# Score matmuls of two units issued together from unit 8 on, under a new written order

## The chip, the cores and the metric

The kernel runs on one core of a Trainium2 chip. The metric is the device time of one execution in microseconds, the median of several runs; a profile of one execution with its trace goes with it.

## The reference

The program computes a linear-attention recurrence and feeds its result to a two-layer perceptron. Inputs are r, k and v of shape (4 batches, 8 heads, 768 steps, 48), a decay w and a bonus u of shape (8, 48), and weights of 384 x 2048 and 2048 x 384.

```python
for t in range(S):
    cur = einsum('bhd,bhe->bhde', u * k_t, v_t)
    y_t = einsum('bhd,bhde->bhe', r_t, state + cur)
    state = w * state + einsum('bhd,bhe->bhde', k_t, v_t)
x = y as (4*768, 8*48)
h = x @ w_in
g = where(h >= 1, h, where(h <= -1, 0, (h + 1)**2 / 4))
out = g @ w_out
```

## The kernel before

**Tiling.** The 768 steps are cut into six chunks of 128. A unit is one chunk of one batch, all eight heads, so there are 24 units; unit i is chunk i // 4 of batch i % 4. Two units make a block (12 blocks), and a block's 256 rows go through the perceptron together: layer 1 in eight groups (`L1:m:n`, each two feature tiles of 128, so six matmuls of 256 columns), the activation `sm:m:n` on ScalarE (ACT), and layer 2 in eight steps for each of the two units (`L2:m:u:n`, two matmuls of 384 columns each), then the copy `oc:m:u` out of PSUM and the store `so:m:u`. The first two blocks run layer 1 by single units (`L1:m:n:u`, twelve matmuls of 128 columns).

**A unit's own work.** Loads `ld:K`, `ld:R`, `ld:V` (line 278) on the queue of SyncE (SP). K and R are weighed with powers of the decay (`Kw`, `Rw`, line 282) into one of five buffers. Both are transposed: by TensorE (PE) and a copy for units below 8 (`trp`, `trc`), by a DMA on SP's queue from unit 8 on (`tr`, line 315). `at:i` (function `scores`, line 317) makes the 128 x 128 scores of the eight heads: eight matmuls, alternating between partitions 0 to 47 and 64 to 111, of 48 rows each, into two PSUM tiles A0 and A1. `mk:i:0` and `mk:i:1` (line 326, VectorE, DVE) mask them into bf16. `y:i` multiplies the masked scores with V and, from the second chunk on, adds K/R's product with the carried state. The diagonal term of u is a product of K, u and R (`KU1`, `KU2`), a reduction to one number per head (`dg:i`, line 297) and eight multiply-adds in `x:i` (line 354, DVE; below unit 6 it is `VD` and one more matmul). `xp`, `xT` turn x for layer 1 (from unit 14 on by DMA). `st`, `Ta`, `Td`, `Tb` update the state for the unit four later. `xs` and `nsq`, `ns`, `nm`, `nx`, `flag` bound the range of h; if the bound fails, a slower exact path runs behind.

**PSUM.** There are eight banks: two for layer 1 (`ps_h`), two for layer 2 (`ps_o`), and four (`ps_a`) taken in turn by everything else: `trp`, `at` (two of them), `y`, `xp`, `st`. A tile takes the bank of the one allocated four before it, and its first matmul waits until that one has been read.

**What sets the order.** Each engine executes its instructions in the order in which they are written, and that order is a string, `ORDER`: its tokens are taken one after the other (line 638), each emits its operation on its engine, and `@DVE`, `@ACT`, `@POOL` behind a token moves it to another engine than its usual one (POOL is GpSimd). `warm*n` emits n idle matmuls that keep PE busy while it has nothing else to do. The table of `op(...)` calls carries estimated costs, needs and due times for a planner that wrote the string; when the kernel is built only the engine and the function of each are used. The weights come in quarters on POOL's queue (`gi`, `go`, lines 465 and 470), each held back by a small copy until a named load has landed; `li` and `lo` emit nothing.

In the order before, each unit's `at` stands alone, with one exception: `at:21 at:22` follow each other but for operations of other engines between them.

Of the kernel before, what the change touches and what calls it, by code (L numbers as in the profile page):

```python
# [16 lines left out]
w u ld:K:0 ld:K:1 ln warm*12 ub tab:K ld:R:0 Kw:0 wt uc ld:V:1 tab:R KU1:0 dec ld:R:1 gi:0 ld:V:0 Rw:0 KU2:0  # L17
warm*41 trp:0 ld:R:2 trc:0@DVE gi:1 li:0 dg:0 warm*11 at:0 Vb:0 mk:0:1 VD:0@POOL st:0 mk:0:0 gi:2 ld:K:2
Ta:0:1 warm*12 y:0 Ta:0:0 Tb:0:1 Rw:1 Tb:0:0 ld:V:2 Kw:1 x:0@DVE warm*17 xp:0 xs:0 li:2 gi:3 trp:1 xT:0
trc:1 Kw:2@DVE warm*2 L1:0:0:0 Rw:2 KU1:1@DVE sm:0:0:0 li:1 warm*7 at:1 KU2:1 mk:1:0 KU1:2 warm*7 L1:0:2:0  # L20
dg:1 mk:1:1 li:3 Vb:1 sm:0:2:0 trp:2 KU2:2@DVE trc:2 VD:1 st:1 dg:2 Vb:2 L1:0:1:0 Ta:1:0 ld:K:3 y:1 VD:2
sm:0:1:0 at:2 Ta:1:1 x:1 ld:K:4 mk:2:1 st:2 Tb:1:0 xs:1 L1:0:3:0 mk:2:0 ld:R:3 go:0 Tb:1:1 xp:1 Ta:2:0
sm:0:3:0 Ta:2:1 ld:V:3 warm*2 y:2 xT:1 Kw:4 x:2@DVE Tb:2:0 ld:R:4 Tb:2:1 go:1 warm*9 L1:0:1:1 xs:2 xp:2 lo:0
sm:0:1:1 L1:0:0:1 go:2 L1:0:2:1 sm:0:0:1 Rw:4 xT:2 L1:0:3:1 Kw:3 sm:0:2:1 lo:1 trp:4 sm:0:3:1 Rw:3@POOL
L1:1:0:0 trc:4@DVE L1:1:1:0 KU1:3 sm:1:0:0 L2:0:1:0 sm:1:1:0 L2:0:0:0 lo:2 go:3 at:4 L2:0:1:1 mk:4:1 KU1:4
L1:1:2:0 mk:4:0 trp:3 sm:1:2:0 KU2:4 L2:0:1:2 lo:3 L2:0:1:3 trc:3 L1:1:3:0 KU2:3 dg:4 sm:1:3:0 Vb:3 dg:3
warm*6 L2:0:1:4 L2:0:1:5 ld:K:5 L2:0:0:1 VD:3@POOL L2:0:0:2 at:3 ld:V:4 L2:0:0:3 mk:3:0 L2:0:0:4 st:3
L2:0:1:6 mk:3:1 ld:K:6 L2:0:1:7 KU1:5 L2:0:0:5 Ta:3:0 L2:0:0:6 Ta:3:1 ld:R:5 Tb:3:0 L2:0:0:7 Vb:4 oc:0:1 y:3
Tb:3:1 VD:4 L2:1:0:0 ld:V:5 x:3 L2:1:0:1 oc:0:0 xs:3 L2:1:0:2 Kw:5@DVE st:4 ld:R:6 y:4 Rw:5 xp:3 x:4
L2:1:0:3 KU2:5 Ta:4:1 ld:V:7 L2:1:0:4 xT:3@DVE xs:4 L2:1:0:5 Ta:4:0 trp:5 Vb:5 dg:5 ld:R:7 L1:1:2:1 Td:4  # L30
trc:5 VD:5 xp:4 ld:V:6 st:5 L1:1:0:1 Kw:6 xT:4@DVE sm:1:2:1 Ta:5:0 L2:1:0:6 Ta:5:1 ld:K:7 sm:1:0:1 at:5
Rw:6@DVE L1:1:3:1 Tb:4:0 KU1:6 mk:5:1 Tb:4:1 ld:R:8 L1:1:1:1 sm:1:3:1 mk:5:0 Td:5 trp:6 ld:K:8 sm:1:1:1
KU2:6@DVE L2:1:1:0 L2:1:0:7 Vb:6@ACT Vb:7 y:5 ld:K:10 trc:6 oc:1:0 Rw:7 L2:1:1:1 x:5@DVE L2:1:1:2 so:0:1
Tb:5:0 Kw:7 L2:1:1:3 dg:6 st:6 Tb:5:1 ld:K:9 L2:1:1:4 xs:5 Ta:6:1 xp:5 KU1:7 at:6 Ta:6:0 xT:5 so:0:0
L2:1:1:5 mk:6:1 L2:1:1:6 ld:V:8 Kw:8 L2:1:1:7 mk:6:0 st:7 L1:2:0 so:1:0 KU2:7 oc:1:1 L1:2:4 ld:R:9 sm:2:0
Ta:7:1 y:6 Td:6 Ta:7:0 sm:2:4 dg:7 L1:2:1 Rw:8 ld:V:9 Tb:6:1 L1:2:3 sm:2:1 KU1:8 x:6 so:1:1 L2:2:1:0 sm:2:3
trp:7 ld:R:10 L1:2:2 Tb:6:0 KU2:8 trc:7 L1:2:5 tr:8 Vb:8 dg:8 xp:6 sm:2:2 Td:7 L2:2:0:0 xT:6@DVE L2:2:0:1
sm:2:5 Rw:9@DVE at:7 ld:K:11 xs:6 st:8 Kw:9 L2:2:1:1 mk:7:1 L1:2:6 ld:R:11 mk:7:0 Kw:10 L1:2:7 sm:2:6 Ta:8:0
ld:V:10 L2:2:0:2 sm:2:7 KU1:9@DVE L2:2:0:3 y:7 Vb:9 Ta:8:1 tr:9 L2:2:1:2 KU2:9 Tb:7:1 x:7 L2:2:1:3 Tb:7:0
L2:2:0:4 L2:2:1:4 Td:8 L2:2:0:5 ld:R:13 L2:2:0:6 Rw:10 dg:9 xs:7 at:8 xp:7 ld:K:12 mk:8:1 L2:2:0:7 Vb:10  # L40
xT:7 L2:2:1:5 Kw:11 mk:8:0 st:9 L2:2:1:6 ld:V:11 L2:2:1:7 Ta:9:0 L1:3:1 Rw:11 Ta:9:1 ld:K:13 oc:2:1 y:8
sm:3:1 L1:3:0 KU1:10 oc:2:0 Tb:8:0 tr:10 x:8 L1:3:2 sm:3:0 KU2:10 at:9 Tb:8:1 L1:3:3 sm:3:2 Td:9 ld:R:12
dg:10 xs:8 L2:3:0:0 KU1:11 L1:3:4 mk:9:1 sm:3:3 ld:V:12 st:10 mk:9:0 Vb:11 xp:8 sm:3:4 L2:3:1:0 L1:3:5
KU2:11@DVE so:2:1 xT:8 Kw:12 Ta:10:0 ld:K:14 L2:3:0:1 sm:3:5 Ta:10:1 y:9 dg:11 L1:3:6 Td:10 Tb:9:0 tr:11 x:9
Tb:9:1 L1:3:7 Rw:12 sm:3:6 L2:3:1:1 sm:3:7 at:10 KU1:13 ld:V:13 L2:3:1:2 xs:9 mk:10:1 L2:3:0:2 Kw:13 xp:9
so:2:0 st:11 mk:10:0 L2:3:1:3 L2:3:1:4 ld:V:14 xT:9@DVE Vb:12 L2:3:0:3 Ta:11:1 L2:3:0:4 Rw:13 Ta:11:0 y:10
ld:R:14 L1:4:0 Tb:10:1 x:10 Td:11 Tb:10:0 L1:4:1 Vb:13 sm:4:0 tr:12 at:11 Kw:14 sm:4:1 L1:4:2 mk:11:1 xs:10
KU1:12 L2:3:0:5 ld:K:15 mk:11:0 L1:4:3 sm:4:2 KU2:12 st:12 xp:10 ld:R:15 sm:4:3 Ta:12:0 L1:4:5 Ta:12:1 xT:10
Rw:14 y:11 dg:12 ld:V:15 sm:4:5 L1:4:4 x:11 Tb:11:1 Td:12 L2:3:1:5 tr:13 sm:4:4 L1:4:6 Vb:14 Tb:11:0 KU2:13
L2:3:0:6 sm:4:6 at:12 L2:3:1:6 xs:11 tr:14 KU1:14 xp:11 dg:13 L1:4:7 xT:11 mk:12:1 KU1:15 L2:3:1:7 sm:4:7  # L50
L2:3:0:7 mk:12:0 ld:K:16 st:13 L1:5:0 Rw:15@DVE ld:R:16 L1:5:2 KU2:14 oc:3:1 sm:5:0 y:12 oc:3:0 sm:5:2
ld:V:16 L1:5:3 Kw:15 Ta:13:1 Tb:12:1 Ta:13:0 L2:4:0:0 sm:5:3 x:12 L2:4:0:1 so:3:1 Td:13 L2:4:0:2 so:3:0
Vb:15 at:13 Tb:12:0 ld:K:17 Kw:16 L1:5:1 mk:13:0 xs:12 L2:4:1:0 L2:4:1:1 Rw:16 dg:14 ld:V:17 sm:5:1 L2:4:1:2
mk:13:1 L2:4:1:3 L2:4:0:3 KU1:16 ld:R:17 L2:4:1:4 st:14 L1:5:4 Ta:14:1 KU2:15 ld:K:18 Ta:14:0 y:13 sm:5:4
at:14 Vb:16 x:13 tr:15 Tb:13:0 L2:4:1:5 Kw:17 Tb:13:1 L2:4:0:4 L1:5:5 mk:14:0 L2:4:0:5 Vb:17 xs:13 ld:R:18
L1:5:6 KU2:16 mk:14:1 sm:5:5 xp:13 L2:4:0:6 ld:V:18 dg:15 xT:13 xp:12 Td:14 L2:4:1:6 dg:16 sm:5:6 y:14 Rw:17
tr:16 L1:5:7 xT:12 x:14 Tb:14:1 KU1:17 L2:4:1:7 sm:5:7 st:15 st:16 L2:4:0:7 ld:K:19 Tb:14:0 KU2:17 L1:6:0
Ta:15:0 xs:14 oc:4:0 at:15 ld:R:19 KU1:18 oc:4:1 sm:6:0 L2:5:0:0 L1:6:1 Ta:15:1 xp:14 mk:15:0 L2:5:1:0 Td:15
sm:6:1 L1:6:2 mk:15:1 Kw:18 so:4:1 L2:5:1:1 sm:6:2 dg:17 L2:5:1:2 so:4:0 Vb:18 L2:5:1:3 Ta:16:1 ld:V:19 y:15
KU1:19 Ta:16:0 L2:5:0:1 Tb:15:1 x:15 at:16 Tb:15:0 ld:K:20 Rw:18 L1:6:3 L2:5:0:2 tr:17 sm:6:3 KU2:18@DVE  # L60
L2:5:0:3 L1:6:4 xs:15 Kw:19 mk:16:1 L2:5:0:4 nsq:0 dg:18 L2:5:1:4 xp:15 Td:16 L2:5:0:5 mk:16:0 st:17 KU2:19
sm:6:4 L1:6:5 Ta:17:0 tr:18 Ta:17:1 L2:5:1:5 sm:6:5 Vb:19 L2:5:0:6 ns:0 L1:6:6 Rw:19 ld:V:20 dg:19 y:16
sm:6:6 L2:5:1:6 Kw:20 x:16 L1:6:7 Tb:16:0 ld:R:20 Tb:16:1 L2:5:0:7 Td:17 sm:6:7 L2:5:1:7 KU1:20 at:17
ld:K:21 nsq:1 oc:5:1 st:18 L1:7:0 mk:17:0 oc:5:0@ACT ld:R:21 L1:7:1 mk:17:1 xs:16 Vb:20 st:19 L2:6:1:0 xp:16
# [36 lines left out]
def kernel(  # L101
# [126 lines left out]
    t = {}  # L228
# [461 lines left out]
```

## Time and profile before

| | |
|---|---|
| median of 5 runs | 182.57 us (182.2 to 183.2) |
| the profiled execution's own time | 183.74 us |
| its span | 181.8 us |
| PE busy | 168.9 us, 93% |
| DVE busy | 121.5 us, 67% |
| POOL busy | 108.4 us, 60% |
| ACT busy | 105.7 us, 58% |
| masks, A to AT (line 326) | 48 of 683 ns |
| x's multiply-adds (line 354) | 144 of 257 ns |
| score weight loads (line 322) | 192, PE idle 4.9 us in 17 places before them, released by nothing seen ("issue") |

The page divides the span into 40 slices and shows the busy share of each in tenths. Its chain of work follows the execution back from its last instruction to what released each step. The timeline lists neighbouring instructions of one kind as one row: start, length to the last one's end, and how often. Matmuls overlap, so the distance between two starts says more about what one costs than its own length. A wait's releaser is inferred; "issue" means that no other engine was seen to release it.

### The profile page before, as it was taken

The page shows a single profiled execution, that of the slowest core. Times are in us where ns is not written, and L with a number is a line of the kernel's source. Part 1 is how long each engine was busy: PE and PEld are TensorE (multiplying, and loading weights), DVE is VectorE, ACT ScalarE, POOL GpSimd, SP SyncE. Part 2 cuts the span into 40 slices and gives each one's busy share as a digit, 9 for nine tenths or more (in the row PEclk, how much of TensorE's full clock was granted, in tenths as well). Part 3 has the DMA queues.
Part 4 walks back from the last instruction along what each step waited for, and adds up shares of the span by engine and source line. Part 5 has one row for each costly group of instructions (what it writes and reads, how often), then busy time and mean ns, then how long its engine had stood idle before and what let it go on. Part 6 is the DMA issues. An engine that isn't in the chain of part 4 may idle for free.

```text
span 181.8 us, 4899 instructions
## 1 busy us (share of the span) xinstructions
PE 168.9 (93%) x1891; PEld 130.2 (72%) x1891; DVE 121.5 (67%) x330; ACT 105.7 (58%) x225; POOL 108.4 (60%) x151
## 2 busy tenths in 40 slices
PE   5987686999999999999999999999999999999970
PEld 3976576767878777787778777777777776877750
DVE  2257773559996999979868899889879674100220
ACT  3406296526869548588738568777947451764200
POOL 7787489663999697999988997932940000000000
PEclk9999999999999999999999999999999999999999
DMA  4999979999989799699999888979972032110221
GB/s 99 218 190 205 190 125 198 188 198 194 227 197 195 161 219 192 140 207 140 246 208 172 199 163 167 232 154 170 238 162 79 4 86 66 40 50 0 73 86 36
DMA packets 103424, 27.79 MB, mean 153 GB/s; under 512 B 96481, under 2 KB 103394, under 8 KB 103394
## 3 DMA queue, kind: packets, MB, share of 16 engines
q1 hardware_dynamic: 99538, 24.16, 65.6%
q0 software_dynamic: 3712, 3.15, 10.8%
q8 instruction: 17, 0.28, 0.7%
q14 instruction: 13, 0.11, 0.2%
q10 hardware_dynamic: 144, 0.10, 0.2%
HBM read 20.65 MB, written 4.72 MB: 139 GB/s over the span
## 4 chain that ended last, share of the span: by engine, by line
PE 80%; SPq 12%; DMA 4%; DVE 1%; issue 0%; ACT 0%
PE o_p L432 35%; PE h_p L401 32%; SPq L278 12%; PE A L322 4%; DMA R<-in_r_dram 4%; PE y L337 2%; PE y L334 2%; PE st L378 2%; PE tr L306 1%; PE xp L362 1%; DVE RKW L282 1%; PE y L343 0%; SPq L243 0%; PE n_p L488 0%; PE o_p L240 0%
## 5 line engine op out<-in xcount | busy, mean ns | idle before, releaser
L412 ACT ACTIVATE gT<-h_p 128x512 bf16<-128x512 f32 x96 | 56.8, 596 | 39.3 <-PE h_p L401 37.5
L401 PE MATMUL h_p<-xT,w_in_sb 128*128 128x256 bf16 (+1 forms) x672 | 75.1, 257 | 2.2 <-DMA w_in_sb<-in_moe_w_in_dram 1.8
L432 PE MATMUL o_p<-w_out_sb,gT 128*128 128x384 bf16 (+1 forms) x400 | 75.9, 320 | 0.0
L401 PEld LDWEIGHTS <-w_in_sb 128*128 128x128 bf16 x672 | 56.8, 98 | 12.6 <-DMA w_in_sb<-in_moe_w_in_dram 1.9
L432 PEld LDWEIGHTS <-gT 128*128 128x128 bf16 x400 | 36.4, 98 | 15.5
L326 DVE TENSOR_TENSOR AT<-A,umask 128x512 bf16<-128x512 f32 x48 | 31.3, 683 | 8.4 <-PE A L322 8.3
L354 DVE SCALAR_TENSOR_TENSOR x<-Vb,dg,y 128x48 bf16<-128x48 bf16 x144 | 26.7, 257 | 3.8 <-PE y L337 3.6
L182 DVE COPY o_sb<-o_p 128x384 f32<-128x384 f32 (+1 forms) x20 | 10.6, 541 | 19.9 <-PE o_p L432 19.7
L282 POOL TENSOR_TENSOR RKW<-K,Winv 128x384 bf16<-128x384 f32 x21 | 21.6, 1033 | 3.6 <-DMA K<-in_k_dram 1.9
L293 POOL TENSOR_TENSOR KU<-KU,R 128x384 f32<-128x384 f32 x20 | 20.2, 1014 | 4.3 <-DVE KU L290 2.8
L182 ACT CAST Tbd<-T 48x192 bf16<-48x192 f32 x40 | 13.9, 348 | 15.2 <-DVE T L386 10.2
L290 POOL TENSOR_TENSOR KU<-K,u_bc 128x384 f32<-128x384 f32 x22 | 21.9, 1000 | 0.0
L372 ACT ACTIVATE x<-x 128x384 bf16<-128x384 bf16 x24 | 12.5, 521 | 5.1 <-DVE x L354 3.7
L282 POOL TENSOR_TENSOR RKW<-R,Wpow 128x384 bf16<-128x384 f32 x14 | 14.0, 999 | 0.8 <-DMA R<-in_r_dram 0.8
L182 POOL CAST Vb<-V 128x384 bf16<-128x384 f32 x22 | 11.3, 517 | 5.2 <-DVE x L354 2.5
L282 DVE TENSOR_TENSOR RKW<-R,Wpow 128x384 bf16<-128x384 f32 x10 | 9.0, 897 | 7.4 <-DMA R<-in_r_dram 7.3
L297 DVE TENSOR_REDUCE dg<-KU 128x8 f32<-128x384 f32 x24 | 13.0, 545 | 1.4 <-POOL KU L293 1.3
L389 POOL TENSOR_TENSOR T<-T,wc 128x192 f32<-128x192 f32 x16 | 9.4, 590 | 6.1 <-DVE T L384 6.1
L384 DVE TENSOR_TENSOR T<-T,st 48x192 f32<-48x192 f32 x32 | 11.2, 350 | 2.6 <-PE st L378 2.1
L240 PE MATMUL w_p<-ident 128*128 128x128 bf16 x120 | 11.1, 261 | 0.0
L240 PEld LDWEIGHTS <-ident 128*128 128x128 bf16 x126 | 10.1, 119 | 0.3
L322 PEld LDWEIGHTS <-RK 48*128 48x128 bf16 x192 | 5.4, 94 | 6.0 <-issue 4.9
(74 smaller groups left out, 146.2 us busy)
## 6 DMA issues: line engine op xcount, KB each, us to landing
K<-in_k_dram SPq DMA_DIRECT2D x24, 192.0 KB, 3.7
R<-in_r_dram SPq DMA_DIRECT2D x24, 192.0 KB, 3.7
V<-in_v_dram SPq DMA_DIRECT2D x24, 192.0 KB, 4.0
out_dram<-o_sb SPq DMA_DIRECT2D x23, 192.0 KB, 2.2
w_in_sb<-in_moe_w_in_dram POOLq DMA_DIRECT2D x4, 384.0 KB, 7.8
w_out_sb<-in_moe_w_out_dram POOLq DMA_DIRECT2D x4, 384.0 KB, 8.1
RK<-RKW SPq DMA_TRANSPOSE x16, 3.9
w_bc<-in_w_dram SPq DMA_DIRECT2D x1, 192.0 KB, 3.6
```

What stands on the lines that cost most here:

```text
L182: (eng.copy if eng is nc.scalar else eng.tensor_copy)(to, src)
L240: mm(spare[0][:, d_out:], ident, ident, start=False, stop=False, skip_group_check=True)
L278: nc.sync.dma_start(out=t[name, i], in_=src[b, :, c * C : (c + 1) * C, :].rearrange("h s d -> s h d"))
L282: at_engine((name + "w", i)).tensor_mul(RKW[i % RING["W"]][:, off : off + H, 0:D], t[name, i], tab)
L290: at_engine(("KU1", i)).tensor_mul(t["KU", i], t["K", i], u3)
L293: at_engine(("KU2", i)).tensor_mul(t["KU", i], t["KU", i], t["R", i])
L297: nc.vector.reduce_sum(t["dg", i], t["KU", i], axis=AX)
L326: nc.vector.tensor_mul(t["AT", i, s], t["A", i][s], umask4)
L354: nc.vector.scalar_tensor_tensor(x[:, h * D : (h + 1) * D], t["Vb", i][:, h, :], t["dg", i][:, h : h + 1], t["y", i][:, h, :], op0=ALU.mul ...
L401: mm(h_p[:, f, :], w_in_sb[:, kk, (nf * n + f) * 128 : (nf * n + f + 1) * 128], xT[m][:, :, kk, :] if u_ is None else xT[m][:, u_, kk, :], ...
L412: nc.scalar.activation(g, h_p, AF.Square, bias=0.5, scale=0.5)
L432: mm(t["o", m, u, part_], t["g", m][:, f, u * C : (u + 1) * C], w_out_sb[:, f, e], start=(f == 0), stop=(f == nN - 1),)
```

## The change

Three edits outside the order, and a new order. `PAIR = 8` is added. From unit 8 on there is no `at` of a single unit: `at:8`, `at:10` and so on emit `scores` of a unit and of the next one (the two units of a block), sixteen matmuls into four PSUM tiles, so that they take the whole `ps_a` pool. `dg` gets 12 buffers instead of 4. The order is another string throughout.

```diff
-    PE_T, PE_X, PE_D, ONE = 8, 14, 6, 2
+    PE_T, PE_X, PE_D, ONE, PAIR = 8, 14, 6, 2, 8
...
-        t["dg", i] = work.tile([128, H], F32, name="dg", tag="dg", bufs=4)
+        t["dg", i] = work.tile([128, H], F32, name="dg", tag="dg", bufs=12)
...
+    RTs = {}
+    def at_key(i):
+        return ("at", i if i < PAIR else i - i % 2)
+
+    def scores_of_two(i):
+        scores(i)
+        scores(i + 1)
...
-        op(("at", i), "PE", 0.45, (scores, i), [RT], d + 3, [("a", [("mk", i, s)]) for s in range(2)])
+        RTs[i] = RT
+        if i < PAIR:
+            op(("at", i), "PE", 0.45, (scores, i), [RT], d + 3, [("a", [("mk", i, s)]) for s in range(2)])
+        elif i % 2:
+            op(at_key(i), "PE", 0.66, (scores_of_two, i - 1), [RTs[i - 1], RT], d + 1,
+               [("a", [("mk", z, s)]) for z in (i - 1, i) for s in range(2)])
```

The order's string, in the places that the prediction speaks of. The start, old and new:

```diff
-w u ld:K:0 ld:K:1 ln warm*12 ub tab:K ld:R:0 Kw:0 wt uc ld:V:1 tab:R KU1:0 dec ld:R:1 gi:0 ld:V:0 Rw:0 KU2:0
+w u ld:K:0 ld:K:1 ln warm*12 ub tab:K ld:R:0 Kw:0 wt uc ld:R:2 tab:R gi:0 dec ld:V:1 Kw:1 ld:R:1 Rw:0 KU1:0
...
-sm:0:1:1 L1:0:0:1 go:2 L1:0:2:1 sm:0:0:1 Rw:4 xT:2 L1:0:3:1 Kw:3 sm:0:2:1 lo:1 trp:4 sm:0:3:1 Rw:3@POOL
+xs:2 xp:2 sm:0:1:1 Rw:4 xT:2 warm*3 L1:0:2:1 Rw:3@POOL sm:0:0:1 lo:1 trp:4 sm:0:2:1 Kw:3 L1:0:3:1 trc:4@DVE
...
-warm*6 L2:0:1:4 L2:0:1:5 ld:K:5 L2:0:0:1 VD:3@POOL L2:0:0:2 at:3 ld:V:4 L2:0:0:3 mk:3:0 L2:0:0:4 st:3
+L1:1:2:0 KU2:4 mk:4:0 trp:3 lo:3 sm:1:2:0 L1:1:3:0 KU2:3 trc:3 dg:4 L2:0:1:2 L2:0:1:3 Vb:3 sm:1:3:0 L2:0:1:4
```

In the new order, the surroundings of trp:7, of L1:3:0 with the first pair, of the pair 12 and 13, and of L1:5:7:

```
+Ta:7:1 L2:1:1:7 ld:V:8 KU2:7 xT:5 trp:7 at:6 trc:7 Td:6 so:1:0 oc:1:1 L1:2:0 Kw:8 ld:R:9 mk:6:0 L1:2:4
...
+L2:2:1:5 oc:2:0 Vb:10 L2:2:1:6 L2:2:1:7 Kw:11 ld:V:11 L1:3:3 oc:2:1 L1:3:4 Td:9 sm:3:3 ld:K:13 KU1:10 sm:3:4
+L1:3:0 tr:10 Rw:11 at:8 sm:3:0 L1:3:2 mk:8:1 KU1:11 L1:3:1 so:2:1 sm:3:2 mk:8:0 ld:V:12 L2:3:0:0 Vb:11
...
+L2:4:1:2 sm:4:7 y:11 Vb:14 xT:10 L2:4:1:3 x:11 ld:V:18 KU2:14 L2:4:1:4 Tb:11:1 L2:4:0:1 Tb:11:0 L2:4:0:2
+Kw:15 L2:4:0:3 ld:R:16 L2:4:0:4 dg:14 xs:11 at:12 Rw:15@DVE ld:V:16 L2:4:0:5 Td:13 mk:12:1 L2:4:0:6 L2:4:0:7
+Vb:15 so:3:1 mk:12:0 Kw:16 so:3:0 mk:13:0 xp:11 ld:K:17 st:14 xT:11 L2:4:1:5 mk:13:1 Rw:16 y:12 ld:V:17
...
+sm:5:1 L1:5:2 x:13 Vb:16 xs:12 st:15 Kw:17 L1:5:3 sm:5:2 ld:R:17 xp:12 st:16 KU2:16 sm:5:3 oc:4:1 L1:5:4
+Ta:15:0 Tb:13:0 ld:R:18 L1:5:5 dg:15 Tb:13:1 KU1:17 sm:5:4 dg:16 xp:13 tr:16 sm:5:5 Vb:17 L1:5:7 Ta:15:1
```

Apart from position, these change engines: Vb:1 (POOL to ACT), KU2:18 and Rw:22 (DVE to POOL), oc:9:0 (DVE to ACT).

## The prediction

> **What bounds the kernel now.** I read the page first, then the chain that ended last, then the timeline of TensorE (PE).
>
> ```profile
> span 181.8 us, 4899 instructions
> ...
> PE   5987686999999999999999999999999999999970
> ...
> PEclk9999999999999999999999999999999999999999
> ```
>
> From the eighth slice to the last but two PE is at nine tenths or more, at full granted clock. The chain says from when on:
>
> ```profile
> 23.12 6.60 DMA R<-in_r_dram
> 29.74 1.17 DVE RKW L282
> 30.96 0.40 PE tr L306 x4
> ...
> 104.77 0.33 PE A L322 x8
> 105.10 0.76 PE h_p L401 x6
> 105.86 0.65 PE o_p L432 x4
> ...
> 137.38 0.55 PE A L322 x16
> 137.93 0.43 PE o_p L432 x2
> 138.36 1.31 PE h_p L401 x12
> ```
>
> Up to 29.74 us it is a load (R of unit 4) and its weighing; from 30.96 to 176.15 us it is PE alone. To see whether PE ever waits there I took the distance from one start to the next (slot) of each form in the timeline: 0.056 us for 128 columns, 0.109 for 256, 0.1625 for 384, 0.026 for 48, 0.043 for 96. All PE work behind 30.96 then adds up to: layer 1 52.4 + 5.4, layer 2 62.5, scores 8.8, y 8.3, state 2.9, turns of K/R 2.0, turns of x 1.9, warming 0.3, norms and flag 0.8, in all 145.2; 30.96 + 145.2 = 176.2 against 176.15. There is no stall in 145 us. So every PE microsecond removed behind 31 us is worth one, and every stall that the new order brings costs one. The remaining 5.6 us to the span's end are the last copy and store, left as they are. The profiled execution took 183.74 us around a span of 181.8; the median of the runs is 182.57. I form a difference on the trace and apply it to the median.
>
> **Part 1, the score matmuls (removed switches).** A group of eight 48-row matmuls holds PE for 0.33 us from its start to the next operation's start, and itself starts 0.10 late: in the chain the six h_p or two o_p behind or around a group show 0.76 and 0.43 where the same forms show 0.66 and 0.33 elsewhere. Eight back to back need 0.22, so 0.21 of each 0.43 is switching in and out. The trace already holds a pair, at 137.38 (units 21 and 22): sixteen matmuls in 0.55, plus the same 0.10, is 0.65 instead of 0.86. Units 8 to 23 stand in 15 groups now and in 8 afterwards: 7 x 0.21 = **-1.47 us**, all of it on the path.
>
> **Part 2, the warming matmuls.** The order has `warm*6` in the saturated stretch; the new order has none behind trp:4.
>
> ```profile
> 20.77 0.84 PE L401 MATMUL h_p<-xT,w_in_sb 128*128 128x128 bf16 x12 [1.77 <-DMA w_in_sb<-in_moe_w_in_dram]
> ...
> 29.39 0.39 PE L306 MATMUL tr<-ident,RKW 128*128 128x128 bf16 x4
> ...
> 30.96 0.40 PE L306 MATMUL tr<-ident,RKW 128*128 128x128 bf16 x4 [1.19 <-DVE RKW L282]
> ...
> 36.39 0.50 PE L240 MATMUL o_p<-ident 128*128 128x128 bf16 x6
> ```
>
> Six slots of 0.056: **-0.34 us**. Warming before 31 us lies in waits and costs nothing either way.
>
> **Part 3, the start.** The R half of trp:4 waits for R of unit 4, which stays the 14th load on SP's queue. R:2 moves ahead of V:1, R:1 and V:0, the weight quarters go 0, 2, 1, 3, and Vb:1 moves from GpSimd (POOL) to ScalarE (ACT). The quarters' issues come some 1.0, 0, 1.0 and 0.7 us earlier (a 1.0 us product on POOL goes behind the first of them, the other steps are POOL rows of 1.0, 0.5 and 0.8). But the DMA row stands at 9 from 4.5 us on, so what must land before R:4 lands at the same time: I take 0.2 earlier, bounds 0.5 earlier and 0.5 later. What changes is the work in front: L1:0:3:1, twelve 128-column matmuls, 0.67 us, is done before trp:4 now (28.72 to 29.39, the second half of the x24 group) and behind it afterwards. It came free of charge and now lies on the path: +0.67 - 0.2 = **+0.5 us** (bounds +0.2 to +1.2).
>
> That makes PE's gap at trp:4 longer, from 1.2 to some 2 us, up to 2.5 since its earlier groups get their weights sooner. Here a rule speaks against the change: the Trainium skill, "TensorE: Matmul & The Clock Gate", Part 1, says an idle window of about 3.4 us puts the array back to half clock, and a busy window of that length is needed to recover. The trace's row: the longest gap among PE's operations around there is 1.77 us (at 20.77) and the granted clock stays full. By the row the gap costs only itself; by the rule, if it reached the window, some 3.4 us of work at half rate, an estimated +1.7 us. 2 to 2.5 us stays short of it; I take nothing and keep 1.7 for the range.
>
> **Part 4, what waits for the pair.** A pair fills all four `ps_a` banks; the next four takers of that pool (y, st, xp) wait for its masks on VectorE (DVE). "TensorEngine Tiling (Array Packing)", Performance Considerations, says that tiling speeds the array and not the emptying of PSUM. By the rows:
>
> ```profile
> 82.67 1.49 DVE L354 SCALAR_TENSOR_TENSOR x<-Vb,dg,y 128x48 bf16<-128x48 bf16 x8
> 84.48 0.55 DVE L297 TENSOR_REDUCE dg<-KU 128x8 f32<-128x384 f32 x1 [0.32 <-POOL KU L293]
> 84.95 1.28 DVE L326 TENSOR_TENSOR AT<-A,umask 128x512 bf16<-128x512 f32 x2
> 86.14 0.63 DVE L282 TENSOR_TENSOR RKW<-R,Wpow 128x384 bf16<-128x384 f32 x1
> ...
> 168.43 1.47 PE L401 MATMUL h_p<-xT,w_in_sb 128*128 128x256 bf16 x12
> ...
> 169.28 1.25 ACT L412 ACTIVATE gT<-h_p 128x512 bf16<-128x512 f32 x2 [1.36 <-PE h_p L401]
> ```
>
> two masks take 1.28 us (pitch 0.60), four take 2.5, against 0.55 on PE. If the rule held in full, each pair would expose up to 2.0 us, 16 us over eight. By the rows it depends on what stands between: I put the new order on PE's time with the slots above and walked DVE's queue for each pair. At the pairs of 8, 10, 14, 16, 18, 20 and 22 the next taker of a freed bank comes 2.1 us or more behind the pair and its masks fit in front. At 12 it doesn't: y:11 ends near 87.3; DVE then has x:11 (0.15 to start, 1.40), dg:14 (0.46), Rw:15 (0.5 to 0.9), mk:12:1 (0.60), mk:12:0 (0.69), done 3.8 to 4.3 us later, at 91.1 to 91.6; xp:11, which takes the bank of that last mask, is due at 90.86. **+0.3**, at most +0.75.
>
> Two other spots of the new order are too tight. `h_p` has two banks. In the rows at 168.43 the first of two groups is over at 169.09 (half of 1.31), its activation starts at 169.28 and takes 0.60: a bank is free about 0.85 us behind its matmuls. The tightest distance in the old order is 0.98. In the new one L1:3:3, L1:3:4, L1:3:0 stand in a row (distance 0.66: **+0.2**), and L1:5:7 comes 0.83 behind L1:5:4 with two casts of Tbd (0.35 each) ahead of the activation on ACT: **+0.15**. Third, trp:7 takes trp:6's bank, whose copy on ACT (1.0 us) now waits behind xs:5: +0.05 to 0.15, taken as **+0.1**. Sum of part 4: **+0.75** (bounds 0 and 2).
>
> **Part 5, the rest of the moves.** `dg` with 12 buffers only lets reductions run ahead. KU2:18 and Rw:22 go from DVE to POOL (two products of 1.0 us; POOL is busy 17.4 of 20 us from 100 to 120 and has gaps behind); oc:9:0 goes to ACT, whose copies take 0.46, at a place where it idles 0.5 us at a time. Loads are issued 3 us or more before first use as now, except R:16, whose distance of 2.6 us on the nominal clock grows because SP reaches it earlier. A transpose lands in 3.9 us; tr:9, tr:11 and tr:13 stand 5.7, 5.7 and 5.7 us ahead of their pairs. Each of these is hidden behind layer matmuls; without that cover a late transpose or POOL product would delay the pair one for one. I take 0.
>
> **Sum.** -1.47 - 0.34 + 0.5 + 0.75 = -0.56; the walk's ends for part 4 are read from busy-port rows, so I lean 0.1 to the short side: -0.65, 182.57 - 0.65 = **181.9 us**.
>
> **The rivals.** *Clean order.* The walk overrates the stalls and R:4 lands early: -1.47 - 0.34 + 0.4 = -1.4, 181.2 us. For it: the old order has no stall at all with similar distances. Against it: 0.66 and 0.83 lie below any distance shown to work.
>
> *Emptying the banks decides, slower.* Place: the pairs of the stretch 60 to 100 us, where DVE is busy 18.7 and 16.4 of 20 us. A product on DVE takes 0.55 us there or 1.33 (at 70.88), and the walk allows one such 0.4. Price: the next y, st or xp stands in PE's in-order queue and all layer work behind it. Without evacuation stalls the sum is -1.47 - 0.34 + 0.5 + 0.45 = -0.86; at 0.11 us per pair the gain is gone, from 0.18 per pair (1.4 in all) it is slower by 0.3%. At 0.19 per pair it gives 183.2 us. Against it: seven pairs looked covered.
>
> *The start decides.* R:4 later by 1.2 us, or the half clock: +1.2 to 1.7 instead of +0.5, some 183.3 us with the rest as taken. Against it: the load's place and the bytes before it are unchanged.
>
> *The change does not remove the switch* is excluded by the pair at 137.38.
>
> **How the numbers follow.** Likeliest case 0.45 (own range 181.4 to 182.5), clean 0.15, emptying 0.30, start 0.10. 0.3% is 0.55 us, about what a measurement can tell from no change. Faster: 0.33 of the likeliest, all 0.15 of clean: 0.48. Slower: 0.21 of emptying, 0.07 of start: 0.28. Same: the rest, 0.24. The range, with a tenth out at each end, is 181.0 to 183.4.
>
> **What the changed profile would show.** Eight groups of x16 for A, each with 0.55 in the chain; the issue idle of the A weight loads down from 17 to about 10 times; no L240 behind 31 us; PE's gap at the R half of trp:4 about 2 us, at an unchanged 30 to 31 us; a small idle of PE before xp:11 (released by AT L326) and before L1:3:0 and L1:5:7 (by gT L412). Wrong would be: R:4 landing elsewhere, idle before y or st at several pairs, a clock below full, or transposes released late by POOL.

## The result, and the profile after

Over several rounds the two kernels took, the one before and the changed one, medians of 182.98 us (181.27 to 186.53, 79 executions) and 182.54 us (180.31 to 187.01, 42 executions). The ratio of the changed kernel to the one before is **0.9933, 95% interval 0.9915 to 0.9952**: applied to the 182.57 us shown before, 181.35 us, 1.2 us shorter. The ratio leaves out executions more than 1.5% above the fastest of their own kernel, 17 of 42 after and 8 of 79 before, so it has to be read beside the medians, which stand only 0.44 us apart; the last section shows what sets them apart.

The forecast of 181.9 us lies between the two readings, and the direction was right. What it is made of was not: the term for the start rested on a single landing, the half clock was put at nothing, and the end was taken as unchanged. The new thing to see is the width: from the 10% to the 90% quantile it was 181.95 to 184.02 before, and is 180.72 to 184.47 after.

The profiled execution of the changed kernel is one of the long ones, 186.13 us around a span of 184.3. Its page:

```profile
span 184.3 us, 4964 instructions
...
PE   6999893999999999999999999999999999999990
...
PEclk9999998599999999999999999999999999999999
```

Two digits show what is new: PE drops to 3 in the seventh slice, and the granted clock to 8 in the seventh and 5 in the eighth. TensorE's timeline there (start, length, line, operation, and in brackets the wait in front and who ended it):

```profile
28.10 0.39 PE L306 MATMUL tr<-ident,RKW 128*128 128x128 bf16 x4
31.62 0.61 PE L306 MATMUL tr<-ident,RKW 128*128 128x128 bf16 x4 [3.13 <-DVE RKW L282]
32.02 2.77 PE L401 MATMUL h_p<-xT,w_in_sb 128*128 128x128 bf16 x24
```

and VectorE's:

```profile
30.52 1.04 DVE L282 TENSOR_TENSOR RKW<-R,Wpow 128x384 bf16<-128x384 f32 x1 [4.33 <-DMA R<-in_r_dram]
```

TensorE has transposed K of unit 4 at 28.10 and stands idle for 3.13 us, because R of unit 4 landed only at 30.52 and then had to be weighed. The 24 matmuls behind it take 2.77 us from first to last where such a group took 1.50 at 25.44 in the same trace. The stretches of 2 us (busy time of TensorE, its weight loads, VectorE, ScalarE and GpSimd, then the granted clock, the DMA share and GB/s) show why:

```profile
28.00:30.00 2.00, 0.49 (x9) 0.32 (x6) 0.00 (x0) 0.85 (x2) 2.00 (x4) 1.00 1.28 207
30.00:32.00 2.00, 0.38 (x4) 0.39 (x5) 1.04 (x1) 0.00 (x0) 1.98 (x3) 0.69 1.27 194
32.00:34.00 2.00, 2.00 (x22) 2.00 (x20) 0.69 (x1) 0.45 (x1) 2.00 (x3) 0.50 1.27 185
```

From 30.77 to 37.60 us TensorE ran at half clock. Behind that the trace shows what the change was about. There are eight groups of sixteen score matmuls and no `L240` behind 31 us, and the waits list

```profile
PEld L306 <- DVE RKW L282: 3.5, 2, 3.3
PEld L322 <- issue: 2.9, 11, 0.6
```

The 17 idles in front of score weights (4.9 us) have become 11 (2.9 us). The chain around units 12 to 15:

```profile
95.04 0.01 DVE AT L326
95.05 0.14 issue
95.19 0.33 PE st L378 x4
...
100.92 0.35 ACT Tbd L182
101.27 0.02 issue
101.29 0.61 ACT gT L412
101.89 0.04 issue
101.94 1.47 PE h_p L401 x12
103.41 0.17 PE st L378 x4
103.58 0.97 PE o_p L432 x6
104.55 0.55 PE A L322 x16
```

A pair costs its 0.55 us. But behind 31 us the chain is no longer TensorE alone: `st:14` waited for a mask (`AT`), and `L1:5:7` for an activation (`gT`) that stood behind two casts of the state (`Tbd`). A chain without another engine in it was what the kernel before had from 30.96 us on.

### The profile page after: what moved, and what is told of

Read it like the earlier page. It is cut to its first block, busy times and chain, and to the rows that moved or that the text cites. A ratio compares the mean times of both kernels' runs of the same rounds, so it can differ in the third digit from the quotient of the medians.

```text
span 184.3 us, 4964 instructions
## 1 busy us (share of the span) xinstructions
PE 172.7 (94%) x1927; PEld 134.9 (73%) x1927; DVE 116.4 (63%) x327; ACT 106.6 (58%) x227; POOL 109.1 (59%) x152
## 5 line engine op out<-in xcount | busy, mean ns | idle before, releaser
L401 PE MATMUL h_p<-xT,w_in_sb 128*128 128x256 bf16 (+1 forms) x672 | 76.5, 262 | 1.2 <-DMA w_in_sb<-in_moe_w_in_dram 0.9
L401 PEld LDWEIGHTS <-w_in_sb 128*128 128x128 bf16 x672 | 58.7, 101 | 12.4 <-DMA w_in_sb<-in_moe_w_in_dram 1.2
L290 POOL TENSOR_TENSOR KU<-K,u_bc 128x384 f32<-128x384 f32 x22 | 23.4, 1068 | 0.0
L282 POOL TENSOR_TENSOR RKW<-R,Wpow 128x384 bf16<-128x384 f32 x15 | 15.4, 1023 | 1.4 <-DMA R<-in_r_dram 1.4
L182 POOL CAST Vb<-V 128x384 bf16<-128x384 f32 x21 | 10.6, 504 | 5.2 <-DMA V<-in_v_dram 3.3
L240 PE MATMUL w_p<-ident 128*128 128x128 bf16 x162 | 13.4, 250 | 0.0
L389 POOL TENSOR_TENSOR T<-T,wc 128x192 f32<-128x192 f32 x16 | 8.5, 529 | 7.2 <-DVE T L384 7.2
L240 PEld LDWEIGHTS <-ident 128*128 128x128 bf16 x162 | 12.0, 114 | 0.2
L282 DVE TENSOR_TENSOR RKW<-R,Wpow 128x384 bf16<-128x384 f32 x9 | 6.6, 733 | 8.2 <-DMA R<-in_r_dram 8.2
L322 PE MATMUL A<-RK 48*128 48x128 bf16 x192 | 8.4, 220 | 0.4 <-DVE RK L182 0.4
```

Of the source, the lines that this page charges most:

```text
L182: (eng.copy if eng is nc.scalar else eng.tensor_copy)(to, src)
L240: mm(spare[0][:, d_out:], ident, ident, start=False, stop=False, skip_group_check=True)
L282: at_engine((name + "w", i)).tensor_mul(RKW[i % RING["W"]][:, off : off + H, 0:D], t[name, i], tab)
L290: at_engine(("KU1", i)).tensor_mul(t["KU", i], t["K", i], u3)
L401: mm(h_p[:, f, :], w_in_sb[:, kk, (nf * n + f) * 128 : (nf * n + f + 1) * 128], xT[m][:, :, kk, :] if u_ is None else xT[m][:, u_, kk, :], ...
```

## The experiments

Each number of a stretch below is the distance between two rows of one trace: **start** is the start of the R half of `trp:4` (the last four of its eight matmuls; where all eight stand in one row, it is taken as 0.22 us, four times 0.056, behind the start of that row, or in front of the next row if the eight were interrupted), **first pair** the start of `at:8`, **end** the end of the last product.

### The changed kernel again, and its pairs taken apart

`again` is the changed kernel without an edit. `split` puts the second unit's eight score matmuls one step of layer work later, eight times; nothing else is changed.

```diff
     def scores_of_two(i):
         scores(i)
-        scores(i + 1)
+
+    def scores_of_second(i):
+        scores(i + 1)
...
+            op(("at2", i - 1), "PE", 0.45, (scores_of_second, i - 1))
...
-at:8 sm:3:0 L1:3:2 mk:8:1
+at:8 sm:3:0 L1:3:2 at2:8 mk:8:1
```

> The changed kernel once more, for its spread and an undisturbed profile. Theory A (the start decides the spread: TensorE waits at the second half of trp:4 for the load of R of unit 4; where the wait nears 3.3 us the clock drops to half and some 2.3 us are lost): executions spread over more than 2 us, the fast end some 1.5 us below the kernel before, and a profile whose wait there is under 3 us shows full clock throughout. Theory B (the spread is the chip's and has nothing to do with the change): the kernel before spreads as widely in the same rounds. Under both: idle of about 0.3, 0.25 and 0.2 us before st:14, L1:5:7 and L1:3:0, as in the first profile of the changed kernel.

> The changed kernel, but in each of the eight pairs the second unit's scores come one layer operation later than the first's, so each pair switches twice. Theory A (a switch in and out costs 0.21 us on the path, the merging is worth 7 x 0.21): 8 x 0.21 = 1.7 us slower than the changed kernel, less at most 0.3 where the wait before st:14 hides a part. Rival (the merging is worth nothing by itself, the new order brings the gain): within 0.4 us of the changed kernel. Chain: 16 groups of x8 with 0.33 each behind unit 8.

`again` took 181.62 us (15 executions) and `split` 183.34 (22), the kernel before 182.62 in the same rounds; ratios to before 0.9946 (0.9910 to 0.9982) and 1.0005 (0.9975 to 1.0034). First pair to end: 107.23 us in `again`, 108.83 in `split`. Taking the pairs apart costs **1.60 us** on the trace, and the whole gain is gone. TensorE's rows of `split` around units 14 and 15:

```profile
101.34 0.40 PE L321 MATMUL A<-RK 48*128 48x128 bf16 x8
101.67 0.83 PE L400 MATMUL h_p<-xT,w_in_sb 128*128 128x256 bf16 x6
102.43 0.40 PE L321 MATMUL A<-RK 48*128 48x128 bf16 x8
102.76 0.83 PE L400 MATMUL h_p<-xT,w_in_sb 128*128 128x256 bf16 x6
```

Six matmuls of 256 columns fill 0.76 us between two groups, 0.66 elsewhere, and each group holds the array for 0.33: 0.43 for a group alone, as worked out. Eight pairs times 0.21 would be 1.68; the trace gives 0.20 for each.

The start is the other thing that these two traces show. `again`, then `split`:

```profile
28.03 1.48 DVE L282 TENSOR_TENSOR RKW<-R,Wpow 128x384 bf16<-128x384 f32 x1 [2.59 <-DMA R<-in_r_dram]
...
27.35 0.39 PE L306 MATMUL tr<-ident,RKW 128*128 128x128 bf16 x4
29.57 0.40 PE L306 MATMUL tr<-ident,RKW 128*128 128x128 bf16 x4 [1.83 <-DVE RKW L282]
29.80 1.50 PE L401 MATMUL h_p<-xT,w_in_sb 128*128 128x128 bf16 x24
```

```profile
27.07 0.39 PE L305 MATMUL tr<-ident,RKW 128*128 128x128 bf16 x4
29.14 0.60 PE L305 MATMUL tr<-ident,RKW 128*128 128x128 bf16 x4 [1.68 <-DVE RKW L281]
29.52 2.77 PE L400 MATMUL h_p<-xT,w_in_sb 128*128 128x128 bf16 x24
```

R of unit 4 was weighed from 28.03 and 27.64 us here, against 30.52 in the changed kernel's first profile. The 24 matmuls took 1.50 at full clock in `again` and 2.77 in `split`, where the clock was half from 29.18 to 32.60 us. It fell after an idle of 1.68 us in `split` and did not after one of 1.83 in `again`; the last section comes back to this.

### What stands in front of `trp:4`

`l1early` puts `L1:0:3:1` back in front of `trp:4`; `warm40` puts forty warming matmuls there; `r4early` has R of unit 4 loaded sooner; `b_l1late` is the kernel *before* with `L1:0:3:1` moved behind `trp:4`, the one move alone.

```diff
 l1early (of the changed kernel)
-lo:1 trp:4 sm:0:2:1 Kw:3 L1:0:3:1 trc:4@DVE
+lo:1 L1:0:3:1 trp:4 sm:0:2:1 Kw:3 trc:4@DVE
 warm40 (of the changed kernel)
-lo:1 trp:4 sm:0:2:1
+lo:1 warm*40 trp:4 sm:0:2:1
 r4early (of the changed kernel)
-y:1 ld:K:4 at:2 ... y:2 ld:R:4 go:1
+y:1 ld:K:4 ld:R:4 at:2 ... y:2 go:1
 b_l1late (of the kernel before)
-xT:2 L1:0:3:1 Kw:3 sm:0:2:1 lo:1 trp:4 sm:0:3:1
+xT:2 Kw:3 sm:0:2:1 lo:1 trp:4 L1:0:3:1 sm:0:3:1
```

> The changed kernel with L1:0:3:1 moved ahead of trp:4, where the kernel before has it. Theory A: the group's 0.67 us lie in the wait for R of unit 4 again; every execution 0.6 to 0.7 us faster than the changed kernel, the wait shorter by the same, so fewer executions with the half clock and the median more than 0.7 us lower. Rival (R of unit 4 lands early enough in most executions that there is no wait to fill): no difference.

> The changed kernel with 40 idle matmuls (2.2 us) ahead of trp:4. Theory A: they lie in the wait and keep the clock: the fast end stays (or is 0.2 us slower, the first half of trp:4 being later), the slow end goes, so the median falls by 0.5 to 1.5 us; full clock throughout in the profile. Rival (the half clock has another cause, or is rare): the spread stays and the median moves by less than 0.3 us.

> The changed kernel with the load of R of unit 4 two places earlier on SP's queue, ahead of R and V of unit 3. Theory A (the landing of this load sets when TensorE's unbroken work begins, and its varying sets the spread): the wait at trp:4 is gone or below 0.7 us, TensorE starts near 28 us, full clock, the spread below 2 us and the median 1 to 2 us below that of the changed kernel. Rival (the wait moves on to the next load or to the quarters of w_out, whose issues now wait for R and V of unit 3 landing later): less than 0.5 us, with a new idle before L2:0:1:2 to L2:0:1:6.

> The kernel before with L1:0:3:1 moved behind trp:4, as the changed kernel has it; nothing else. Theory A (the group is worth the part of its 0.67 us that lies in the wait for R of unit 4, and a longer wait lets the clock fall more often): 0.2 to 0.7 us slower in the median, more executions above 184.5 us. Rival (TensorE reaches trp:4 later than R of unit 4 in most executions of the kernel before): no difference.

> The kernel before once more, for a second profile of its start. Theory A: R of unit 4 is weighed at some other moment than 29.74 us, within 27.5 to 30.6; TensorE reaches trp:4 at 29 us or later, and the stretch from its second half to the last product is 145.2 us as in the first profile.

`before2` is the kernel before, for a second trace. Measured:

| | this, us | before in the same rounds, us | ratio (95%) | R:4 weighed from | start |
|---|---|---|---|---|---|
| `l1early` | 181.04 | 182.62 | 0.9872 (0.9829 to 0.9915) | 28.84 | 29.51 |
| `warm40` | 182.18 | 182.62 | 0.9967 (0.9936 to 0.9999) | 27.54 | 30.40 |
| `r4early` | 182.04 | 183.00 | 0.9969 (0.9933 to 1.0004) | 25.58 | 27.67 |
| `b_l1late` | 183.66 | 183.00 | 1.0029 (1.0003 to 1.0055) | 29.66 | 31.09 |
| `before2` | 181.93, once | 183.00 | | 28.53 | 29.60 |

First the two that answer the question. In the kernel before the single move of `L1:0:3:1` makes it slower: 0.53 us by the ratio, whose interval only just leaves 1 out, and from start to end 146.00 instead of 145.16 us. Of these 0.84 us 0.67 are the group itself, as foreseen; the other 0.17 lie in the row behind, where three groups of layer 1 now follow each other (36 matmuls in 2.18 us from 31.33, where three times 0.67 would be 2.01). But the old order cannot use an early R. The rows of `before2`, then of `b_l1late`:

```profile
28.53 0.93 DVE L282 TENSOR_TENSOR RKW<-R,Wpow 128x384 bf16<-128x384 f32 x1 [2.21 <-DMA R<-in_r_dram]
...
29.38 0.61 PE L306 MATMUL tr<-ident,RKW 128*128 128x128 bf16 x8
```

```profile
28.40 0.39 PE L306 MATMUL tr<-ident,RKW 128*128 128x128 bf16 x4
31.09 0.40 PE L306 MATMUL tr<-ident,RKW 128*128 128x128 bf16 x4 [2.31 <-DVE RKW L282]
```

In `before2` R was weighed from 28.53, 1.2 us earlier than in the first profile of the same kernel, and `trp:4` runs in one piece without a wait: TensorE itself arrives only at 29.38, as it did there (29.39). In the changed order it arrives between 27.07 and 28.10 and takes what an early R gives, or waits for a late one. Over all the profiles here with its load in the same place of the queue R of unit 4 was weighed from 27.5 to 30.5 us. That fits the greater width, but the move of the group alone does not make it: `b_l1late` stayed within 182.46 to 184.07 us in twelve executions, and none of those above 184.5 us that were expected came. `warm40` fills the gap: no gap and full clock, 181.44 to 183.30 us instead of 180.41 to 183.73 in `again`, but the forty matmuls run over an early R as well (start 30.40 with R weighed from 27.54), and the median is 0.56 us longer instead of the 0.5 to 1.5 us shorter that was expected.

`r4early` moves the load itself. It removes the wait at `trp:4`, and the next one takes its place:

```profile
27.45 0.61 PE L306 MATMUL tr<-ident,RKW 128*128 128x128 bf16 x8
...
35.02 1.46 PE L432 MATMUL o_p<-w_out_sb,gT 128*128 128x384 bf16 x8 [1.10 <-DMA w_out_sb<-in_moe_w_out_dram]
```

TensorE is now ready for a quarter of the second layer's weights before it is there. Start to end is 146.26 us, 1.27 more than in `again`, most of it this wait. An early R did not narrow the times either: 180.62 to 184.53 us, with the granted clock below 0.99 in four of twelve executions. `l1early` shows the same wait with 0.76 us. Its median is 0.58 us below that of `again` in the same rounds, near the 0.67 of the group, but the intervals of the two ratios overlap, and its profile is not the faster one (first pair at 67.81 us, in `again` at 67.33).

### The stalls that the new order brings

`fixes` takes the three late spots apart: one layer 2 step between `L1:3:3` and `L1:3:4`, so that `L1:3:0` has its bank in time, the weighing of R of unit 15 behind the last mask of unit 12, and the two casts `Tb:13` behind the activation that `L1:5:7` waits for.

```diff
-L2:2:1:6 L2:2:1:7 Kw:11 ld:V:11 L1:3:3 oc:2:1 L1:3:4
+L2:2:1:6 Kw:11 ld:V:11 L1:3:3 L2:2:1:7 oc:2:1 L1:3:4
...
-at:12 Rw:15@DVE ld:V:16 L2:4:0:5 Td:13 mk:12:1 L2:4:0:6 L2:4:0:7 Vb:15 so:3:1 mk:12:0 Kw:16
+at:12 ld:V:16 L2:4:0:5 Td:13 mk:12:1 L2:4:0:6 L2:4:0:7 Vb:15 so:3:1 mk:12:0 Rw:15@DVE Kw:16
...
-Tb:13:0 ld:R:18 L1:5:5 dg:15 Tb:13:1 KU1:17 ... tr:16 sm:5:5 Vb:17 L1:5:7
+ld:R:18 L1:5:5 dg:15 KU1:17 ... tr:16 sm:5:5 Tb:13:0 Tb:13:1 Vb:17 L1:5:7
```

> The changed kernel with the three tight spots of its order widened: Rw:15 behind the masks of unit 12, the two casts Tb:13 behind sm:5:5, a step of layer 2 between L1:3:3 and L1:3:4. Theory A (each idle of TensorE behind 31 us costs its length): the 0.34 us before st:14, 0.26 before L1:5:7 and 0.19 before L1:3:0 go, so from the pair of unit 8 to the last product 106.6 us instead of 107.2 (the third lies before that pair), and the time 0.8 us shorter. Rival (the stalls move elsewhere: a later Rw:15 delays the transpose and the pair of 14, or another bank is late next): less than 0.4 us.

181.25 us against 183.00 before, ratio 0.9870 (0.9816 to 0.9924, from four of the six executions; the other two took 184.1 and 185.2 us at a granted clock of 0.987 and 0.981). The trace: `L1:3:0` no longer waits (start to first pair 37.57 us instead of 37.76), `st:14` waits 0.17 instead of 0.34, and `L1:5:7` not at all instead of 0.26. Yet first pair to end is 107.25 us, as in `again` (107.23): what was saved came back 2.5 us later.

```profile
97.24 0.33 PE L378 MATMUL st<-Vb,RKW 128*128 128x96 bf16 x4
97.41 1.14 PE L432 MATMUL o_p<-w_out_sb,gT 128*128 128x384 bf16 x6
98.48 0.97 PE L322 MATMUL A<-RK 48*128 48x128 bf16 x16
```

The pair of units 14 and 15 takes 0.97 instead of 0.62 us: it stops 0.35 us in its middle. My first reading was the transpose of unit 15, issued 0.8 us later since its weighing had been moved. Three more kernels carried these edits together with those of the start; a fourth, `best`, was made to test that reading, with `Rw:15` back in its place:

| | edits to the changed kernel |
|---|---|
| `l1early_fixes` | `l1early` and `fixes` |
| `all3` | `l1early`, `fixes` and `r4early` |
| `all4` | `all3`, and the quarters of w_out released by the landings of K:3, R:4, R:3, V:3 instead of K:3, R:3, V:3, K:4 |
| `best` | `l1early_fixes` without the move of `Rw:15` (`L2:2:1:7` stands between `L1:3:3` and `L1:3:4` here too) |

> The changed kernel with both repairs: L1:0:3:1 ahead of trp:4 and the three tight spots widened. Theory A (both are independent and each costs its length on the path): 0.67 + 0.8 = some 1.4 us below the changed kernel, and from the pair of unit 8 to the last product 106.6 us. Rival (the start's waits are set by transfers, and what is gained behind them is lost there): no more than one of the two, 0.8 us.

> As l1early_fixes, and the load of R of unit 4 two places earlier. Theory A as it stands after the run with the early load (the wait moves to the second quarter of w_out, which then lands near 35 us): no wait at trp:4, an idle of 1.1 us or more before L2:0:1:2, and no gain over l1early_fixes beyond 0.5 us, but fewer executions with the half clock. Rival (that idle was one execution's): 1 us below l1early_fixes.

> As all3, with the quarters of w_out held back by R of unit 4, R of unit 3 and V of unit 3 in place of R and V of unit 3 and K of unit 4, so that the second quarter's issue no longer waits for the load that was moved behind. Theory A: the idle before L2:0:1:2 goes, TensorE's work is unbroken from 28 to 29 us on, 1 us below all3. Rival (the transfers as a whole are late, and the next to wait is the transpose of unit 3 for R of unit 3): an idle at trp:3 or at a later quarter in its place, and no gain.

> The version with three moves, but Rw:15 left where the changed kernel has it; L1:0:3:1 in front of trp:4, L2:2:1:7 between L1:3:4 and L1:3:0, the casts Tb:13 behind sm:5:5. If the stall in the pair of units 14 and 15 (sixteen score matmuls in 0.97 instead of 0.62 us) came from the transpose of unit 15, issued 0.8 us later because its weighing had been moved, then the pair of 14 takes 0.62 again, st:14 waits 0.34 again, and the distance from the first pair to the end of the last product is 107.23 - 0.26 = 106.97 us (107.23 with all three moves, 107.24 in the changed kernel). If the pair's stall has another cause, it stays, and the distance is 107.3. The median, by trace, is 0.2 below that of the version with all three moves: 181.1, with before at 183.0; ratio 0.99. If the landing of R of unit 4 decides alone, no difference to the version with all three moves will be seen in the medians.

| | this, us | before, us | ratio (95%) | first pair to end, us |
|---|---|---|---|---|
| `l1early_fixes` | 181.29 (180.03 to 182.26) | 183.00 | 0.9921 (0.9889 to 0.9953) | 107.23 |
| `all3` | 181.90 (180.84 to 184.15) | 183.00 | 0.9942 (0.9910 to 0.9975) | 107.24 |
| `all4` | 181.67 (178.97 to 183.06) | 183.00 | 0.9847 (0.9757 to 0.9937) | 107.24 |
| `best` | 181.60 (180.38 to 182.55) | 182.58 | 0.9938 (0.9910 to 0.9967) | 107.38 |

The reading fell: in `best` the pair stands still as long (99.20, sixteen in 0.97), with `Rw:15` where it always was, and the stretch is 107.38 instead of the 106.97 expected. The chain of `best` at this place names another cause:

```profile
97.15 0.34 ACT Tbd L182
97.49 0.02 issue
97.51 0.36 ACT Tbd L182
97.87 0.02 issue
97.89 0.61 ACT x L372 x2
98.50 0.37 ACT xT L182
98.87 0.50 ACT gT L412
99.37 0.38 ACT xT L182
99.74 0.04 issue
99.79 0.38 PE A L322 x7
```

It is ScalarE's queue. The two casts that I had put behind the activation now push the copies `xT` out; the second one frees the `ps_a` bank that the second unit's scores take, and the last seven matmuls of the pair go on 0.04 to 0.05 us after it is done. The trace also rules the transpose of unit 15 out: in `best` it was issued at 94.61 and landed 3.9 us later, at 98.5, before the pair began at 99.20; in `fixes` it was issued at 94.41 and landed 3.8 us later, at 98.2, with the pair at 98.48. In `again` the second copy `xT` ends at 99.55, the pair starts at 99.62, and nothing waits. The move of the casts is common to `fixes` and the four kernels of the table, and each has the row of 0.96 or 0.97. So the wait of `L1:5:7` was exchanged for one of the pair: 0.26 for 0.35. No further run undid the casts' move alone in these kernels.

`all3` and `all4` show the start once more. With R early and all else in place TensorE reached the second layer's weights so soon that it waited 2.56 us in `all3`, and the clock was half from 36.30 to 39.71 us:

```profile
36.25 1.11 PE L432 MATMUL o_p<-w_out_sb,gT 128*128 128x384 bf16 x3 [2.56 <-DMA w_out_sb<-in_moe_w_out_dram]
```

With the other release in `all4` the wait was 0.99, as in `r4early`. None of these versions can be told from `l1early` or `fixes` by its ratio; of the four `l1early_fixes` and `best` have the narrowest spreads, 2.2 us.

## Why the prediction was right or wrong

**The switches (part 1, -1.47).** Right. Taking them apart again costs 1.60 us on the trace; with the pair of 21 and 22, which the kernel before had already, eight pairs were worked out at 1.68. So the rival named before `split`, that the new order alone brings the gain, is excluded.

**The warming matmuls (part 2, -0.34).** None is left behind 31 us. It was not tested alone, but together with part 1 it can be seen in the stretch from start to end, at full clock on both sides: 145.16 and 145.14 us in the two traces of before, 144.99 in `again`. The steps say -1.47 - 0.34 + 0.67 for `L1:0:3:1`, and 1.02 for the stalls as they were measured (below), together -0.12; the traces differ by -0.16.

**The stalls (part 4, +0.75).** Right in kind, somewhat too small in size. In the traces of the changed kernel `L1:3:0` waited 0.19 (predicted 0.2) and `L1:5:7` 0.26 (0.15). At the pair of 12 and 13 the wait was 0.34 (0.3), released by a mask as foreseen, but it was `st:14` and not `xp:11` that stood there. `trp:7` (0.1) shows no wait, but `at:6`, the next to be issued, does: its row has 0.50 us in both traces of the changed kernel, where the other groups of eight at full clock have 0.40. ScalarE's copy `xT:5`, behind the copy of `trp:6`, ends there at 52.41 us, which fits the reason given. One more wait of 0.13 stood before `xp:5` and was not foreseen; what it waited for I did not follow. Sum 1.02. The other pairs were covered, as the walk had said, so the rival in which the emptying of the banks decides did not happen.

**The start (part 3, +0.5).** Here the prediction failed. Its two terms were 0.67 for the matmuls moved behind `trp:4`, and a landing of R of unit 4 that is taken 0.2 us earlier than in the one profile. The first is right, as `b_l1late` shows, if a little small there. The second took one landing, 29.74 us, for a constant. It moves between 27.5 and 30.5 us, and with it the sign of the step. That the number came out near is therefore in part luck. What the new order really changed is when TensorE gets there: 27.1 to 28.1 us instead of 29.4. In the profiles an early R gave a start of 28.95 to 29.57 us in the new order, where the two traces of the kernel before have 29.60 and 30.96, and a late one costs the gap. The profile after, with R at 30.52, shows the one side (start 31.62, 0.66 later than before), `fixes` the other (start 28.95, 0.65 earlier than in `before2`).

**What was weighed and put at nothing: the half clock.** The rule of the Trainium skill, "TensorE: Matmul & The Clock Gate", Part 1, was set aside because a gap of 2 to 2.5 us stays short of the window of 3.4 us. This was the other step that failed: the clock was halved after a gap of 3.13 us in the profile after, and also after 1.68 us in `split`, far short of a whole window. From start to first pair, the profile after has 40.56 us and `again` 37.76: it cost 2.8 us there, with two windows at half clock. In `split`, with one, it cost 1.6 (39.37), where the prediction had estimated 1.7 for the case.

**What was left out: the end.** The 5.6 us behind the last product were taken as unchanged. They are 5.68, 5.36 and 5.21 us in the traces of before and of `b_l1late`, and 4.88 and 4.84 us in the two of the changed kernel. In the new order `L2:11:1:2:1` stands behind `oc:11:0`, one matmul more between the last two copies, so that VectorE's copy of the first half starts 1.00 us before ScalarE's of the second instead of 0.82, and the two stores are further apart. In the other runs of the new order it was 4.8 to 5.1 us, but 5.5 in `all4`; the mean is 5.0 over eleven traces of the new order and 5.4 over three of the old. That the later matmul is the cause was not tested alone, and the landing of the last store varies by half a microsecond by itself.

Comparing two traces with R nearly equally early, `again` (span 179.4) and `before2` (180.1), the sum is: start -0.03, stretch -0.15, end -0.52, together -0.7, near the forecast of -0.65 but not by its working. The two readings of the result, -1.2 and -0.44, stand apart by how often the clock was halved (at the end, under "It can be seen in the times"). Why the executions at full clock gain 1.2 us and these two traces 0.7 was not followed; earlier starts, of which `fixes` shows one, would do it.

## What to carry to other kernels

A load that ends a wait in one profile has a spread of its own: look at a second execution before taking its time as a term, and ask which engine will be the later of the two afterwards. Putting two groups of small matmuls that use part of the array side by side was worth what the rows said, 0.21 us for every two groups joined; the price here was four PSUM banks taken at once, which showed as a wait of 0.34 us at one pair of eight. A stall of a quarter microsecond can be moved to its neighbour by the move that removes it, so a fix is read from the length of the whole stretch and not from the row that was mended.

## What was not expected of the hardware

**The length of the gap did not decide the clock; how it lay in a fixed grid did.** Idle of TensorE in front of `trp:4`, and the clock behind it: 1.34 us full (`fixes`), 1.68 half (`split`), 1.83 full (`again`), 2.31 full (`b_l1late`), 3.13 half (the profile after). Halved stretches lasted 3.41 us (`split`, 29.18 to 32.60, and `all3`, 36.30 to 39.71) and 6.83 (the profile after, 30.77 to 37.60), once or twice 3.413. The Trainium skill, "TensorE: Matmul & The Clock Gate", Part 1, says that the window of 3.4 us runs freely and does not begin with the kernel, and the traces agree. In every trace the clock falls behind the last product, and where it had fallen earlier too, the two falls are whole windows apart: 44 times 3.413 us in `split` (29.18 and 179.37), 42 in `all3` (36.30 and 179.66), 45 in the profile after (30.77 and 184.37). So the last fall gives the grid of every execution, and with it TensorE's busy share in each window:

| trace, window (us) | busy share | clock in the window behind |
|---|---|---|
| profile after, 27.36 to 30.77 | 0.31 | half |
| `split`, 175.96 to 179.37 | 0.41 | half |
| `split`, 25.77 to 29.18 | 0.46 | half |
| `l1early`, 173.46 to 176.87 | 0.47 | full |
| before, 17.28 to 20.70 | 0.51 | full |
| `b_l1late`, 26.61 to 30.03 | 0.58 | full |
| `again`, 28.20 to 31.61 | 0.60 | full |

No window of the 14 traces contradicts this: at full clock each with 0.47 or more kept it, and each with 0.46 or less lost it. A halved window that was busy for 0.75 (the profile after, 30.77 to 34.18) did not bring full clock back, and wholly busy ones did. The rule as the prediction cites it asks for an idle window; here one that was busy for 0.46 was idle enough, and the measurement decides. The gap of 1.68 us in `split` lay with 0.16 us of smaller idles in one window; those of `again` and `b_l1late` were cut in two by a boundary. An estimate from these shares: in otherwise unbroken work a gap of 2.0 to 2.5 us puts 1.84 us of idle (0.54 of 3.413) into one window in about half to two thirds of its possible positions. That is the chance that the prediction put at nothing.

**It can be seen in the times.** Of the 46 executions of the changed kernel whose clock is listed, 20 had a mean granted clock below 0.99 and took 182.6 to 187.0 us (median 183.8); the 26 others took 180.3 to 183.6 (median 181.4). Of 111 executions of the kernel before, in the rounds of the experiments, only 14 lay below 0.99 (median 183.6), and the 97 others had a median of 182.65. The two lists come from different rounds, but by them the change is worth about 1.2 us where the clock stays full, which is the ratio's reading, and the more frequent half clock takes most of it back in the median. Layer work or warming in front of `trp:4` goes with fewer such executions: none of 24 in `l1early_fixes` and `best`, none of 14 in `warm40` and one of ten in `l1early`, against five of 15 in `again`, six of 22 in `split` and two of six in `fixes`. With R early as well, where the next wait is longer, it was two of twelve in `all3` and one of six in `all4`.

**A queued load's landing moved by 3 us.** R of unit 4 has the same place on SyncE's queue and the same bytes in front of it in all executions of the changed kernel, and was weighed from 28.03 in one (`again`) and from 30.52 in the other (the profile after), with the page's DMA row at nine tenths from the second slice to the fifth in both. Most of the difference was there when the load was issued: SyncE's row for it starts at 21.92 us in `again` and at 23.47 in the profile after, because the loads ahead of it had held the queue longer; the landing then took 6.1 and 7.0 us. Why the queue was held longer was not followed.
